# Softmax attention and a two-layer MLP: the key layout of the third batch, and every load at the second step

## The chip, the cores and the metric

The kernel runs on one core of one Trainium2 chip. The core's engines have a queue each and run side by side: TensorE (PE, matrix products, results in PSUM), VectorE (DVE), ScalarE (ACT), GpSimd (POOL) and SyncE (SP, which here only issues DMAs). The metric is the device time of one execution in microseconds (us), lower is better.

## The reference

Inputs are float32. There are 8 batches of 12 heads with 448 tokens of 64 numbers; the MLP has a width of 768 and 2048 hidden units.

```python
def _attn_ref(q, k, v):
    scale = 1.0 / np.sqrt(q.shape[-1])
    scores = scale * np.matmul(q, k.transpose(0, 1, 3, 2))
    scores = scores - np.max(scores, axis=-1, keepdims=True)
    attn = np.exp(scores)
    attn = attn / (np.sum(attn, axis=-1, keepdims=True) + 1e-09)
    return np.matmul(attn, v).astype(np.float32)

def _moe_ref(x, w_in, w_out):
    h = x @ w_in
    g = np.maximum(0.01 * h, h)
    return (g @ w_out).astype(np.float32)
# x of the MLP: the attention output of each token, its 12 heads side by side
```

## The kernel before

A unit is one batch and a pair of heads, so there are 8 x 6 = 48 units (NU), six (HP) to a batch; unit u belongs to batch u // 6. For a unit the kernel does the following.

- **Load.** POOL's DMA queue brings q, k and v of two units at a time (L157, `load_soft`) and turns them to bf16 on the way.
- **Cast.** POOL copies them into the layouts that PE needs (`cast`): q and k into one of three buffers `qkb` (L184, or L186 to L188 for the new form of k), v into `v_old` (L190) or `v_sb` (L193 to L195). `v_old` is not a buffer of its own: it lies in `x_mix`.
- **Turn.** q and k are transposed into one of four buffers `qkT`: by PE up to unit 14 (L289, copied out of PSUM by DVE at L293), by a DMA transpose from SP's queue from unit 15 (NPE) on (L271, `dma_transposes`).
- **Scores.** PE multiplies keys with queries (L309 old form, L312 new form) into one of three PSUM buffers ("slots", two heads wide), ACT takes the exponential (L321, L324, L326) into `e`.
- **Rows.** PE multiplies the exponentials with v, which has a column of ones for the sum (`pairs`, L352, old form; `weighted`, L333 and L340, new form); DVE takes the reciprocal and multiplies (L875, L876) and gives x.
- **x is turned** into `xT`, mostly by a DMA transpose from SP's queue (L267).

There are two forms of a unit. In the **old form** (units below HY, here 2 x HP = 12) the 448 keys lie in four chunks of 112, and each chunk is done for both heads: eight score products, four exponentials of 896 columns, 32 products for the rows. In the **new form** the keys lie in three chunks of 128 for both heads, and a rest of 64 keys of each head, which shares one product with the other head's: seven score products, three exponentials of 896 columns and one of 448, 28 products for the rows. The new form needs two loads for k and two for v, and three copies for each cast of k and v.

The tokens go through the MLP in seven ranges (`cuts`: 0, 640, 1152, 1664, 2176, 2688, 3072, 3584). The head (L419) and the neck (L715) do the first layer of range 0; `second(0)` does its second layer (L674, L609); `hidden(i)` (L537) and `second(i)` (L609) do the later ranges. These later products are done with fewer multiplications, from sums and differences of blocks, which DVE makes: `mix_x_part` (L484) writes `x_mix` from `xT` for the next range, in two parts, and the steps L614, L617 keep and join the partial outputs. Outputs are stored from SP's queue (L397).

Attention units are interleaved into the MLP's product stream by a planner, `place`, at the time of building: it holds a model of when slots come free and puts at each step, into PE's fixed order, a **burst** (three chunks' scores and exponentials), a **tail** (the rest chunk), or the rows of a unit. In the old form a burst is the next three chunks in a row, so four bursts are three units; in the new form it is one unit's three chunks, and the tail follows. `plan` says how many bursts each range's second layer takes (6 in `second(0)`), `goals` gives two to the neck. All queues keep the order in which the builder issues, so an instruction that waits holds up what stands behind it on its engine: POOL's casts behind its loads, SP's x turns behind its qkT turns and stores.

Within `second` and `hidden`, `advance` (called at every second or fourth step) casts the next unit and issues the next load, at every second call or, in range 0, at each; `turn_next` issues the next qkT turn. In the neck `feed` does so.

Of the kernel before, what the change touches and what calls it, by code (L numbers as in the profile page):

```python
# [16 lines left out]
def kernel(  # L17
# [9 lines left out]
    nc = tc.nc  # L27

    B, H, S, D = q.shape
    DM, DF = moe_w_in.shape  # L30
    P = 128
    HP = H // 2
    SC = 112
    NSC = S // SC
# [3 lines left out]
    NU = B * HP  # L38
# [40 lines left out]

    NV = 4  # L80
    KC = S // P
    HY = 2 * HP
    v_all = v_pool.tile([P, NV, 2 * KC + 2, D + 1], BF16, name="v")
    v_sb = [v_all[:, i] for i in range(NV)]

# [9 lines left out]
    NQ = 4  # L95
    qkT_all = qk_pool.tile([P, NQ, 2, NSC, P], BF16, name="qkT")
    qkT = [qkT_all[:, i] for i in range(NQ)]
    NB = 3
    qkb_all = cast_pool.tile([P, NB, 2, NSC, 2, D], BF16, name="qkb")
    qkb = [qkb_all[:, i] for i in range(NB)]  # L100
# [16 lines left out]
    h = h_pool.tile([P, MD, (KEEP + 1) * P], BF16, name="h")  # L117
# [15 lines left out]
    for t in (w_in_mix, w_mix):  # L133
        t = t.rearrange("p x k n -> p (x k n)")
# [42 lines left out]
    def cast(u, parts=(0, 1, 2), by=nc.gpsimd.tensor_copy):  # L177
        if u >= NU:
            return
        for x in parts:  # L180
            f = raw[u].pop(x)
            t = qkb[u % NB]
            if x < 2 and (x == 0 or u < HY):
                by(t[:SC, x].rearrange("p so h d -> p h so d"), f)  # L184
            elif x == 1:
                by(t[:, 1, :KC].rearrange("p so h d -> p h so d"), f[:, :, :KC])  # L186
                by(t[:D, 1, KC, 0], f[:D, 0, KC])
                by(t[D:, 1, KC, 1], f[:D, 1, KC])  # L188
            elif u < HY:
                by(v_old[:, u % NV, :, :, :D], f)  # L190
            else:
                t = v_sb[u % NV]
                by(t[:, :2 * KC, :D].rearrange("p (h so) d -> p h so d", h=2), f[:, :, :KC])  # L193
                by(t[:D, 2 * KC, :D], f[:D, 0, KC])
                by(t[D:, 2 * KC + 1, :D], f[:D, 1, KC])  # L195
# [68 lines left out]
    NPE = HP + 9  # L264

    def turn(dst, src):
        nc.sync.dma_start_transpose(out=dst.rearrange("p (c s) -> p c s", s=SC), in_=src)  # L267

    def dma_transposes(u):
        if NPE <= u < NU:  # L270
            nc.sync.dma_start_transpose(  # L271
                out=qkT[u % NQ].rearrange("p i c s -> p (i c) s"),
                in_=qkb[u % NB].rearrange("p i so h d -> p (i so h d)"),
            )
# [5 lines left out]
    def transposes(u, bank=None):  # L280
        if u >= min(NPE, NU):
            return
        n = SC if u < HY else P
        t, flat = qkb[u % NB], qkT[u % NQ].rearrange("p i c s -> p (i c s)")[:, :2 * NSC * n]
        for parts in ((1,), (0,)) if u == 0 else ((0, 1),):
            tr = turn_tile(bank)[:, :2 * NSC * n].rearrange("p (i s) -> p i s", i=2)
            for i in parts:
                for so in range(NSC):
                    nc.tensor.transpose(tr[:, i, ts(so, n)], t[:n, i, so].rearrange("p h d -> p (h d)"), ident[:n, :n])  # L289
            if u == 0 and parts == (0,):  # L290
                stay_warm(5)
            at = slice(parts[0], parts[-1] + 1)
            (nc.scalar.copy if u == 0 and parts == (1,) else nc.vector.tensor_copy)(  # L293
                flat.rearrange("p (i s) -> p i s", i=2)[:, at], tr[:, at]
            )
        if HY - NB <= u < HY:
            nc.vector.memset(qkb[u % NB][:, 1, KC], 0.0)

    sc_t = {}

# [524 lines left out]
    chunk = NSC * HP + 3  # L825
    nxt = HY
    owed_t = []
    rows_done = HP
    to = {"pe": HP + 2, "turn": NPE, "q": HP + 4, "cast": HP + 4, "v": HP + 4, "load": [HP + 8] * 3}
    tick = 0  # L830

    def advance(i):
        nonlocal tick
        tick += 1
        u = to["cast"]
        if u < min(NU, to["turn"] + 2, to["load"][0], to["load"][1]):
            cast(u, (0, 1))
            to["cast"] += 1
        u = to["v"]
        if u < min(NU, rows_done + NV, to["load"][2]):  # L840
            cast(u, (2,))
            to["v"] += 1
        if tick % 2 == 0 or i == 0:
            x = min(range(3), key=lambda x: to["load"][x])
            u = to["load"][x]
            if u < NU and u - 3 < (to["cast"], to["cast"], to["v"])[x]:
                load_soft(u, 2, (x,))
                to["load"][x] += 2

    def turn_next(i):  # L850

        u, full = to["turn"], nxt - len(owed_t)
        left = need[min(i + 2, NR)] - rows_done
        calm = left < 1 or left > 1 and full - rows_done < 2
        if (calm or u <= nxt + 1) and u < min(NU, full + NQ, to["cast"]):
            dma_transposes(u)
            to["turn"] += 1

# [105 lines left out]
            dma_transposes(u + 2 + r)  # L964
            to["turn"] = max(to["turn"], u + 3 + r)

    plan = [6, 6, 6, 6, 6, 4, 0]
    model = {"now": 0.0, "act": 0.0, "free": {}, "ready": {}}

    def place(i, want, soon=0, full=True, calm=True, first=False, lazy=0, keen=NU, cap=NU):  # L970

        free, ready = model["free"], model["ready"]
        done, state = 0, 0
        while True:
            settle_x(model["now"])
            now = model["now"]
            old = chunk < NSC * HY
            last, full_to = ((chunk + 2) // NSC, chunk // NSC) if old else (nxt, nxt - len(owed_t))
            whole = rows_done < full_to
            at = [free.get(id(x), 0.0) for x in slots]  # L980
            u = to["pe"]
            if full and max(want, soon) > done and u <= min(last, NPE - 1) and state == 0:
                transposes(u)
                to["pe"] += 1
                state = 1
                model["now"] += 0.45
                continue
            if want > done and state < 2 and last < NU and not owed_t and turned(last) and rows_done > last - NE and len(slots) == 3 and all(
                x <= now + 0.05 + 0.2 * j for j, x in enumerate(at)
            ):  # L990
                state = 2
                order = list(slots)
                g = chunk // 3 if old else 4 + nxt
                burst(lazy)
                if first:
                    feed(g)
                done += 1
                for x, t in enumerate(order):
                    model["act"] = max(model["act"], now + 0.45 + 0.2 * x) + 0.8
                    free[id(t)] = model["act"] + (0.3, 0.15 + 0.5 * (lazy > 1), 0.15 + 0.5 * lazy)[x]  # L1000
                    if old and (3 * g + x) % NSC == KC:
                        ready[(3 * g + x) // NSC] = model["act"] + 0.1
                model["now"] = now + 0.78
                continue
            u = to["pe"]
            if first and full and state == 0 and u < min(NPE - 1, to["cast"] - 1) and u - NQ < full_to and model["act"] <= now + 0.6:
                transposes(u)
                to["pe"] += 1
                state = 1
                model["now"] += 0.45  # L1010
                continue
            u = rows_done
            if calm and whole and not (lazy and late) and at[0] <= now + 0.05 and ready.get(u, 0) <= now + 0.05 and (
                u <= ((chunk + 5) // NSC if old else nxt + 1) - NE or u < keen
            ) and u < cap:
                t = slots[0]
                rows()
                if first:
                    pay()
                model["now"] = now + (1.08 if u < HY else 1.04)  # L1020
                free[id(t)] = model["now"] + 1.25
                continue
            if owed_t and not late and at[0] <= now + 0.05:
                t, u = slots[0], owed_t[0]
                tail(lazy)
                model["act"] = max(model["act"], now + 0.45) + 0.43
                free[id(t)] = model["act"] + 0.15 + 0.5 * (lazy > 1)
                ready[u] = model["act"] + 0.1
                model["now"] = now + 0.19
                continue  # L1030
            return done

    def second(i):
# [4 lines left out]
        for c in range(len(spots(i)[1])):  # L1038
            whole = c < plain(i)
            for x, _ in enumerate((plain_pair if whole else block_pair)(i, c)):  # L1040
                fine = 1 if whole else 2
                if x % (2 * fine) == 0:
                    advance(i)
                if c or x:
                    model["now"] += 0.65 / fine
                left -= place(i, left, calm=whole or x not in ((1, 2, 3) if i == 5 else (1, 2)), keen=need[min(i + 2, NR)], cap=NU if all(summed) else need[i + 2])
# [44 lines left out]
        pass  # L1091
    for i in range(1, NR):
        for step, _ in enumerate(hidden(i)):
            advance(i)
            if owed_t and step == 0:
                tail()
            if step % 4 == 2 and rows_done < nxt:
                rows()
            turn_next(i)
        model.update(now=0.0, act=2.3, free={id(x): 0.9 if cuts[i + 1] - cuts[i] == 4 * P and i + 1 < NR else 1.2 for x in slots}, ready={})  # L1100
        second(i)
# [30 lines left out]
```

## Time and profile before

| What | us |
|---|---|
| Median of three runs | 388.58 |
| Lowest and highest of them | 385.97, 389.38 |
| The profiled execution, its own time | 386.52 |
| Its span in the trace | 384.70 |
| PE busy in the span | 373.3 (97%) |
| ACT, DVE, POOL busy | 253.1, 230.8, 189.8 |
| PE in 0 to 61, idle | 4.1 of 61.0 |
| PE in 61 to 108.28 (end of the head, the neck, `second(0)`), idle | 3.4 of 47.3 |
| PE in 344.60 to 384.70, idle | 3.4 of 40.1 |

PE busy counts matrix products, whose ends are modelled from a pipeline; a row of products one behind the other counts as busy without a gap. PE's granted clock was 1.00 in each of these stretches.

### The profile page before, as it was taken

Reading aid. Unit: us, or ns where it says so; the run is one execution under the profiler, and the core shown is the slowest. Engines: PE = TensorE matmul, PEld = TensorE weight load, DVE = VectorE, ACT = ScalarE, POOL = GpSimd, SP = SyncE. Lnnn points to the kernel's source line nnn. Section 1 sums busy time; section 2 is a strip of 40 time slices with the busy share of each in tenths; the row PEclk is TensorE's granted clock in tenths of the full one; section 3 lists DMA queues with packets and bytes.
Section 4 is the critical chain, followed back from the end, with each engine's and each line's share of the span. In section 5 each row is a group of like instructions: output and inputs, shape, how many; then the busy total and the mean of one; then the engine's idle time right before and its main releaser. Section 6 shows DMA issues by size and latency. Waiting matters only on the chain.

```text
span 384.7 us, 9849 instructions
## 1 busy us (share of the span) xinstructions
PE 373.3 (97%) x3910; PEld 261.8 (68%) x3910; DVE 230.8 (60%) x491; ACT 253.1 (66%) x391; POOL 189.8 (49%) x403
## 2 busy tenths in 40 slices
PE   7999999989989999999999999999999999999996
PEld 3665557755578665786568875678756896668854
DVE  5663948453675836668467574565745665474854
ACT  6988875666638787378783787827878378608700
POOL 8996952898779629481285903848036100000000
PEclk9999999999999999999999999999999999999999
DMA  9999999889989929992699913999239700331022
GB/s 162 197 200 203 178 203 167 99 114 184 183 116 179 140 55 152 224 133 38 78 174 209 140 19 76 165 213 142 26 69 182 164 14 2 76 97 43 2 77 86
DMA packets 100349, 47.92 MB, mean 125 GB/s; under 512 B 65872, under 2 KB 96976, under 8 KB 100304
## 3 DMA queue, kind: packets, MB, share of 16 engines
q0 software_dynamic: 40864, 22.47, 48.0%
q1 hardware_dynamic: 59376, 24.81, 33.4%
q8 instruction: 30, 0.49, 0.5%
q14 instruction: 15, 0.12, 0.1%
q10 hardware_dynamic: 64, 0.02, 0.0%
HBM read 45.61 MB, written 11.01 MB: 147 GB/s over the span
## 4 chain that ended last, share of the span: by engine, by line
PE 72%; DMA 15%; POOL 9%; issue 2%; DVE 1%; ACT 0%; POOLq 0%; DVEq 0%
PE g L609 28%; PE g L537 14%; PE sc L537 14%; PE sc L312 6%; PE sc L340 6%; DMA w_out_sb<-in_moe_w_out_dram 4%; DMA w_in_sb<-in_moe_w_in_dram 3%; DMA xT<-x 3%; DMA w_mix<-in_v_dram 2%; POOL qkb L184 2%; PE sc L333 2%; DMA w_in_mix<-in_v_dram 2%; DMA fk<-in_k_dram 1%; POOL fv L157 1%; POOL qkb L186 1%
## 5 line engine op out<-in xcount | busy, mean ns | idle before, releaser
L321 ACT ACTIVATE e<-sc 128x896 bf16<-128x896 f32 (+1 forms) x144 | 123.7, 932 | 35.1 <-PE sc L312 29.7
L609 PEld LDWEIGHTS <-h 128*128 128x128 bf16 x632 | 59.2, 98 | 46.8 <-issue 11.7
L609 PE MATMUL g<-w_out_sb,h 128*128 128x384 bf16 x416 | 78.8, 326 | 0.4 <-DVE o L614 0.4
L184 POOL COPY qkb<-fq 112x512 bf16<-112x512 bf16 x36 | 24.0, 667 | 84.4 <-DMA qkT<-qkb 72.6
L526 ACT ACTIVATE h<-c 128x512 bf16<-128x512 f32 (+1 forms) x72 | 43.6, 613 | 25.0 <-DVE c L552 15.7
L537 PEld LDWEIGHTS <-w_in_sb 128*128 128x128 bf16 x576 | 54.3, 98 | 5.9
L537 PEld LDWEIGHTS <-w_in_mix 128*128 128x128 bf16 x432 | 41.2, 98 | 4.1
L875 DVE RECIPROCAL rec<-sc 112x8 f32<-112x8 f32 x42 | 8.7, 207 | 55.4 <-PE sc L340 41.4
L312 PE MATMUL sc<-qkT 64*128 64x448 bf16 (+1 forms) x252 | 39.3, 352 | 1.5 <-DMA qkT<-qkb 1.5
L609 PE MATMUL g<-w_mix,h 128*128 128x384 bf16 (+1 forms) x208 | 39.1, 323 | 1.4 <-DVE o L617 1.4
L340 PE MATMUL sc<-v,e 128*128 128x65 bf16 x864 | 40.0, 193 | 0.0
L340 PEld LDWEIGHTS <-e 128*128 128x128 bf16 x864 | 37.4, 98 | 2.1 <-issue 0.5
L614 DVE COPY o<-g 128x384 f32<-128x384 f32 x49 | 27.1, 553 | 11.2 <-PE g L609 10.8
L333 PE MATMUL sc<-v,e 128*128 128x130 bf16 x144 | 31.7, 220 | 0.2 <-POOL v L195 0.2
L617 DVE TENSOR_TENSOR o<-o,g 128x384 f32<-128x384 f32 x39 | 21.6, 554 | 14.9 <-PE g L609 14.1
L876 DVE TENSOR_TENSOR x<-sc,rec 112x512 bf16<-112x512 f32 x42 | 29.0, 692 | 1.7 <-DVE rec L875 0.3
L549 ACT COPY c<-g 128x512 f32<-128x512 f32 (+1 forms) x12 | 6.8, 570 | 34.6 <-PE g L537 34.6
L537 PE MATMUL sc<-xT,w_in_sb 128*128 128x256 bf16 (+1 forms) x216 | 28.5, 268 | 0.0
L537 PE MATMUL g<-xT,w_in_sb 128*128 128x256 bf16 (+1 forms) x216 | 28.5, 268 | 0.0
L157 POOL DMA_DIRECT2D fv<-in_v_dram x36 | 22.2, 624 | 9.2 <-POOL v L195 3.3
L193 POOL COPY v<-fv 128x384 bf16<-128x384 bf16 x36 | 18.6, 518 | 12.2 <-issue 8.3
L312 PEld LDWEIGHTS <-qkT 64*128 64x128 bf16 (+1 forms) x252 | 11.3, 94 | 16.9 <-issue 10.1
(129 smaller groups left out, 669.1 us busy)
## 6 DMA issues: line engine op xcount, KB each, us to landing
fq<-in_q_dram POOLq DMA_DIRECT2D x18, 224.0 KB, 5.7
w_in_sb<-in_moe_w_in_dram POOLq DMA_DIRECT2D x4, 768.0 KB, 11.3
w_out_sb<-in_moe_w_out_dram POOLq DMA_DIRECT2D x4, 768.0 KB, 15.4
out_dram<-o SPq DMA_DIRECT2D x7, 336.0 KB, 3.9
fk<-in_k_dram POOLq DMA_DIRECT2D x18, 128.0 KB, 5.1
fv<-in_v_dram POOLq DMA_DIRECT2D x18, 128.0 KB, 4.7
out_dram<-o SPq DMA_DIRECT2D x8, 288.0 KB, 3.3
fk<-in_k_dram POOLq DMA_DIRECT2D x18, 96.0 KB, 5.0
```

The lines of the kernel that those rows point to most:

```text
L157: nc.gpsimd.dma_start(out=t[p, :n, :, :so].rearrange("p u h so d -> p (u h) (so d)"), in_=(q, k, v)[x][b, hs, keys].rearrange("h (p so) d ...
L184: by(t[:SC, x].rearrange("p so h d -> p h so d"), f)
L312: nc.tensor.matmul(ps[:, j, :S].rearrange("p (so s) -> p so s", so=NSC), t[p, 1, c], t[p, 0, :, :SC], start=True, stop=True,)
L321: nc.scalar.activation(e[:, :, c, :], ps[:n, :, :S], AX.Exp, scale=scale)
L333: nc.tensor.matmul(ps, e[:, EM + qc * SC:EM + qc * SC + P], vt[:, 2 * KC:].rearrange("p j d -> p (j d)"), start=True, stop=False, skip_gro ...
L340: nc.tensor.matmul(ps[:, j * (D + 1):(j + 1) * (D + 1)], e[:, at:at + P], vt[:, j * KC + c], start=False, stop=(c == KC - 1), skip_group_c ...
L526: nc.scalar.activation(hs[:, m:m + 2, cols], x.rearrange("p (m t) -> p m t", m=2), AX.Prelu, alpha=0.01)
L537: nc.tensor.matmul(ps[:, j * nh:(j + 1) * nh], w[:, kk, ts(j, P)], x[:, kk], start=(first and j == 0 and kk == 0), stop=(kk == KH - 1), sk ...
L609: nc.tensor.matmul(ps[:, cols], x[:, m], w[:, m], start=(first and m == 0), stop=(m == MH - 1), skip_group_check=True,)
L614: by(o[:, at], ps[:, :NW])
L617: nc.vector.tensor_add(o[:, at], o[:, at], ps[:, :NW])
L876: nc.vector.tensor_mul(x, ps[:, :, :, :D], rec.to_broadcast([SC, 2, 2 * NP, D]))
```

## The change

HY becomes 3 x HP = 18: the six units 12 to 17, the third batch, are taken in the old form. With it:

- their q and k are turned with 112 partitions: on PE for 12 to 14, and by a DMA transpose of 112 partitions and eight blocks for 15 to 17;
- the zeroing of the rest chunk in the three `qkb` buffers, ahead of the first units in the new form, moves from DVE (behind PE's transposes of units 9 to 11) to POOL (into the casts of k of units 18 to 20);
- `turn_next` counts chunks instead of units as long as bursts are in the old form;
- `second(0)` takes eight bursts instead of six: six bursts are left of units 13 to 17 when the neck is done, and then units 18 and 19 follow, as they did before;
- loads are issued at every second call of `advance` in range 0 too.

```diff
--- before.py
+++ after.py
@@ -79,7 +79,7 @@
 
     NV = 4
     KC = S // P
-    HY = 2 * HP
+    HY = 3 * HP
     v_all = v_pool.tile([P, NV, 2 * KC + 2, D + 1], BF16, name="v")
     v_sb = [v_all[:, i] for i in range(NV)]
 
@@ -183,6 +183,8 @@
             if x < 2 and (x == 0 or u < HY):
                 by(t[:SC, x].rearrange("p so h d -> p h so d"), f)
             elif x == 1:
+                if u < HY + NB:
+                    nc.gpsimd.memset(t[:, 1, KC], 0.0)
                 by(t[:, 1, :KC].rearrange("p so h d -> p h so d"), f[:, :, :KC])
                 by(t[:D, 1, KC, 0], f[:D, 0, KC])
                 by(t[D:, 1, KC, 1], f[:D, 1, KC])
@@ -267,7 +269,12 @@
         nc.sync.dma_start_transpose(out=dst.rearrange("p (c s) -> p c s", s=SC), in_=src)
 
     def dma_transposes(u):
-        if NPE <= u < NU:
+        if NPE <= u < HY:
+            turn(
+                qkT[u % NQ].rearrange("p i c s -> p (i c s)")[:, :2 * S],
+                qkb[u % NB][:SC].rearrange("p i so h d -> p (i so h d)"),
+            )
+        elif NPE <= u < NU:
             nc.sync.dma_start_transpose(
                 out=qkT[u % NQ].rearrange("p i c s -> p (i c) s"),
                 in_=qkb[u % NB].rearrange("p i so h d -> p (i so h d)"),
@@ -293,8 +300,6 @@
             (nc.scalar.copy if u == 0 and parts == (1,) else nc.vector.tensor_copy)(
                 flat.rearrange("p (i s) -> p i s", i=2)[:, at], tr[:, at]
             )
-        if HY - NB <= u < HY:
-            nc.vector.memset(qkb[u % NB][:, 1, KC], 0.0)
 
     sc_t = {}
 
@@ -829,7 +834,7 @@
     to = {"pe": HP + 2, "turn": NPE, "q": HP + 4, "cast": HP + 4, "v": HP + 4, "load": [HP + 8] * 3}
     tick = 0
 
-    def advance(i):
+    def advance():
         nonlocal tick
         tick += 1
         u = to["cast"]
@@ -840,7 +845,7 @@
         if u < min(NU, rows_done + NV, to["load"][2]):
             cast(u, (2,))
             to["v"] += 1
-        if tick % 2 == 0 or i == 0:
+        if tick % 2 == 0:
             x = min(range(3), key=lambda x: to["load"][x])
             u = to["load"][x]
             if u < NU and u - 3 < (to["cast"], to["cast"], to["v"])[x]:
@@ -849,10 +854,11 @@
 
     def turn_next(i):
 
-        u, full = to["turn"], nxt - len(owed_t)
+        u, old = to["turn"], chunk < NSC * HY
+        full, last = (chunk // NSC, (chunk + 2) // NSC) if old else (nxt - len(owed_t), nxt)
         left = need[min(i + 2, NR)] - rows_done
         calm = left < 1 or left > 1 and full - rows_done < 2
-        if (calm or u <= nxt + 1) and u < min(NU, full + NQ, to["cast"]):
+        if (calm or u <= last + 1) and u < min(NU, full + NQ, to["cast"]):
             dma_transposes(u)
             to["turn"] += 1
 
@@ -964,7 +970,7 @@
             dma_transposes(u + 2 + r)
             to["turn"] = max(to["turn"], u + 3 + r)
 
-    plan = [6, 6, 6, 6, 6, 4, 0]
+    plan = [8, 6, 6, 6, 6, 4, 0]
     model = {"now": 0.0, "act": 0.0, "free": {}, "ready": {}}
 
     def place(i, want, soon=0, full=True, calm=True, first=False, lazy=0, keen=NU, cap=NU):
@@ -990,7 +996,7 @@
             ):
                 state = 2
                 order = list(slots)
-                g = chunk // 3 if old else 4 + nxt
+                g = chunk // 3
                 burst(lazy)
                 if first:
                     feed(g)
@@ -1040,7 +1046,7 @@
             for x, _ in enumerate((plain_pair if whole else block_pair)(i, c)):
                 fine = 1 if whole else 2
                 if x % (2 * fine) == 0:
-                    advance(i)
+                    advance()
                 if c or x:
                     model["now"] += 0.65 / fine
                 left -= place(i, left, calm=whole or x not in ((1, 2, 3) if i == 5 else (1, 2)), keen=need[min(i + 2, NR)], cap=NU if all(summed) else need[i + 2])
@@ -1091,7 +1097,7 @@
         pass
     for i in range(1, NR):
         for step, _ in enumerate(hidden(i)):
-            advance(i)
+            advance()
             if owed_t and step == 0:
                 tail()
             if step % 4 == 2 and rows_done < nxt:
```

## The prediction

> **What bounds the kernel now.** I read the busy time by stage first, cut where the matrix products change (head to 61, neck and first range to 108.28, range 1, ranges 2 to 5, last range). PE is nearly always at work:
>
> ```profile
> core 0: us, PE busy (x) PEld busy (x) DVE busy (x) ACT busy (x) POOL busy (x), PEclk, DMA share, GB/s
> 0.00:61.00 61.00, 56.92 (x729) 34.25 (x730) 35.89 (x94) 49.55 (x68) 47.40 (x82) 1.00 1.25 192
> 61.00:108.28 47.28, 43.84 (x461) 28.93 (x459) 27.94 (x60) 28.19 (x42) 35.80 (x71) 1.00 1.02 144
> 108.28:157.48 49.20, 48.76 (x493) 34.89 (x492) 30.57 (x60) 33.78 (x52) 33.24 (x76) 1.00 1.00 133
> 157.48:344.60 187.12, 187.12 (x1949) 136.06 (x1947) 113.82 (x236) 125.86 (x201) 73.42 (x174) 1.00 0.72 109
> ```
>
> From 157.48 to 344.60 PE has no idle time at all. PE's order in the built changed kernel is the same as before up to 53 us (two transposes there become 112 wide) and again from 108.28 on. So what the change can win lies in the second window, where PE is idle for 47.28 - 43.84 = 3.44 us. The waits of that window, from 61 to 110, name them (total, times, longest):
>
> ```profile
> DVE x_mix L484 <- DMA xT<-x: 1.9, 1, 1.9
> ...
> PE sc L312 <- DMA qkT<-qkb: 1.5, 2, 1.2
> ...
> PE g L609 <- DVE o L617: 1.4, 1, 1.4
> ...
> PE sc L333 <- POOL v L195: 0.2, 1, 0.2
> PE sc L289 <- ACT e L321: 0.2, 1, 0.2
> ```
>
> 1.5 + 1.4 + 0.2 + 0.2 = 3.3: nearly all of it. The 1.5 us are the scores of units 16 (1.25, at 86.80) and 17 (0.26, at 91.71), whose transposed q and k landed late. The timeline of POOL shows why: in the chain of waits POOL follows POOL without a break from 65.39 to 88.9.
>
> ```profile
> 65.39 0.73 POOL L184 COPY qkb<-fq 112x512 bf16<-112x512 bf16 x1 [10.57 <-PE g L715]
> ...
> 79.87 1.33 POOL L184 COPY qkb<-fq 112x512 bf16<-112x512 bf16 x1
> ...
> 82.01 0.27 POOL L188 COPY qkb<-fk 64x64 bf16<-64x64 bf16 x1
> ...
> 84.67 1.46 POOL L188 COPY qkb<-fk 64x64 bf16<-64x64 bf16 x1
> ```
>
> The casts of unit 16 end at 82.28, its DMA transpose is issued at 82.30 and scores start at 86.80; unit 17's casts end at 86.13 and its scores start at 91.71. The 1.44 us of L609 are DVE's: it waits 1.89 us for a transposed x (unit 16's, issued at 100.09, behind an output store on SP), and the join that PE needs is queued behind.
>
> **PE work.** Scores: a full group of three chunks takes 0.67 us (chain rows, six matmuls), a rest 0.18 (83.91 to 84.09). Old form: four chunks 4/3 x 0.67 = 0.89; new form 0.67 + 0.18 = 0.85. Weighted sums: 32 matmuls from 52.12 to 53.15, 1.03 us; 28 from 95.94 to 96.91, 0.97. So +0.04 and +0.06 for each of six units: +0.6 us, on the path. PE transposes of 112 and 128 both take 0.49 (45.78 to 46.27, 60.48 to 60.97): 0.
>
> **ACT.** 4 x 0.966 against 3 x 0.920 + 0.556: +0.55 a unit, +3.3 us. In 64.30 to 108.28 ACT is busy 27.42 of 43.98 us, so 16.6 us of idle time hide it; without that cover it would cost all 3.3. The order now holds ten groups and two rests there instead of eight and eight.
>
> **POOL.** A unit's casts: q and k in two copies of 0.667 and v in one of 0.618, 1.95 us, against 0.667 + (0.549 + 0.288 + 0.314) + (0.518 + 0.239 + 0.273) = 2.85. Loads of a pair: three issues of about 0.71 (2.15) against 0.717 + 4 x 0.627 = 3.22. Six units and three pairs: 5.4 + 3.2 = 8.6 us less. Three memsets come in from DVE, where they took 0.11; no POOL memset of that size is in the view, so 0.1 to 0.7 each (the smallest by DVE's, the largest by a copy four times as wide), taken as 0.3. They stand ahead of the k casts of units 18 to 20, when POOL is ahead; so 0.
>
> Now the chain from 65.39, which starts when q of unit 14 lands behind the w_out loads (the same bytes, so the same time): casts of 14 and 15 2.67, v 0.62, loads of 16/17 2.15, two v 1.24, loads of 18/19 3.22 (new form), casts of 16 1.33, v 0.62, casts of 17 1.33, and about 1 us of gaps: 14.2. Unit 16 is ready at 77.6 (was 82.28), unit 17 at 79.6 (was 86.13).
>
> At 84.67 L188 took 1.46 us (median 0.233) beside two two-input DVE operations (L440, 85.02 to 86.04), and L187 1.44 at 90.59 beside the next two. If that hits unit 17's casts once more, it is ready at 80.8; the margin below bears it.
>
> **When PE needs it.** I lay the new PE order from 64.3 with the rows' rates (0.0835 a neck matmul, 0.163 a 384-wide one): groups at 64.3, 68.0, 73.8, 76.5, 81.8, 84.5, 88.8, 93.4, 96.0, 100.2. Unit 16's first chunk is second in the sixth group (84.7), unit 17's third in the seventh (89.2). With a landing of 4.5 (the six x turns of 66 to 100 had 4.1 to 6.2, a qkT turn of this stage a median of 5.4) they land at 82 and 84. So 1.5 us go. The margins are 2.6 and 5 us.
>
> SP's queue: x of units 13 and 14 now stands behind the turns of 16 and 17, and x of 16 and 17 stands behind the turn of 20, which waits for the seventh group. Weighted sums of 16 come at 92, its x is turned at 93.4 and lands by 98.5 to 99.6; DVE reaches the mixing at about 100. So the 1.44 us of L609 go too. The 0.2 of v and most of the 0.2 of the slot go by the shorter POOL chain. Kept: 0.4 us for new small waits of this order (bound 0 to 1). The loads that came every step and now come every second step move to range 1, where POOL waits long for qkT turns (5.85 us at 144.07): 0.
>
> **Sum.** -(3.4 - 0.4) + 0.6 = -2.4 us. The profiled execution took 386.52 (span 384.70 and 1.82 around it), so 384.1. The median shown is 388.58, 2.06 more, and the runs go from 385.97 to 389.38. If that surplus lies outside this window, the changed median is 386.2; if it is more of the same waits, 384.1. I take the middle, 385.0 (-0.9%).
>
> **Rivals.** (1) The idle time only moves. v of the old form lies in x_mix, which the mixing for range 1 overwrites, and unit 17's weighted sums now come 5.3 us before range 1 (before: 97.10 to 108.28, 11.2). From their end to the first product with the mixed second part is 5.3 + 1.0 + 4 x 0.66 = 8.9 us. My chain is 1.2 (DVE) + 5 (turn) + 1 (three mixing steps) = 7.2. For: before, the last mixing step ended at 109.8, 12.7 us after those sums. Against: there, two stores and another turn were ahead on SP. If it stays at 12.7 minus the last step's 0.3, PE stalls 3.5 and all is given back: 387.6 against the profiled base of 386.5; with the surplus of the median up to 389.7. Chance 0.18.
>
> The mixing steps L484 took 0.248 to 0.485 us over all their shapes, so rows show them held up by 0.2 at most. The Trainium skill, page "SBUF — State Buffer", section "Who interferes with whom", says that a DVE instruction with two SBUF inputs and a GpSimd instruction that reads SBUF shut each other out for a whole instruction. The POOL copies above agree (1.2 us lost each time). By that rule each of the three steps could wait for a POOL cast of 0.667, the chain would be 9.2 instead of 7.2, PE would stall 0.3, and my sum would be -2.1; it is a part of why this rival keeps 0.18.
>
> (2) Slower: the turn of 112 partitions by 8 blocks. No row has it. x turns are 112 by 4 and land in 4.7, qkT turns 128 by 8 in 5.4, so I took that range; the worst landing of an x turn in the view of xT is 10.9. Above 7.1 us unit 16 is late. At 10.9 each, one behind the other, unit 17 would land at 77.6 + 21.8 = 99.4 instead of 89.2: PE stalls 10.2, 394.3. It decides for "slower by 1%" from about 10 us. Against: x turns with 112 partitions are not slow, and 896 rows of 256 bytes are moved instead of 1024. With other waits of the same place (ACT with three score buffers), chance 0.17.
>
> (3) The change does not what it says: the order does show six units in four chunks and the single loads, so 0.03 for no effect of any sort.
>
> **How the numbers follow.** My case has 0.62; its times are 384.1 to 386.2, with up to 1.6 less if the kept waits and the PE terms are smaller, 382.5. About 1% is what a measurement of this kernel can tell: below 384.7 is faster, above 392.5 slower. I give 0.42 of the 0.62 to faster, because the surplus of the median is most likely in the POOL-paced stage, and 0.20 to same; rival 1 is same (0.18), rival 2 slower (0.17), the rest is split. Range 382.5 to 389.7, my case and rival 1 (0.80).
>
> **What would show it.** Right: from 61 to the end of the first range PE's idle time falls from 3.44 to under 1 us, no wait of scores for qkT and none of L609 for the join, PE busy there up 0.6, ACT up 3, POOL's casts of units 16 and 17 done by about 80, and every later stage unchanged to 0.1 us. Wrong: scores waiting for a qkT turn with landings over 7 us (rival 2), or range 1's products waiting for DVE's mixing (rival 1), or idle time in the windows that I took as unchanged.

## The result, and the profile after

The changed kernel takes 383.51 us (median of six runs, 381.98 to 386.25), the kernel before 388.35 us (median of six, 385.97 to 389.38). The ratio of the means is 0.9889 (that of the medians 0.9875) with a 95% interval of 0.9845 to 0.9933: faster by 1.1%. The ratios in this document leave out executions that are more than 1.5% longer than the fastest of the same kernel. The forecast was 385.0 with a range of 382.5 to 389.7. The profiled execution of the changed kernel took 383.68 us, its span is 381.3 us.

The busy time by stretch comes first. The cuts lie at the first scores of the neck and at the first product of range 1 (L537 before, L542 now), since these two points can be found to a hundredth in every kernel of this study. Columns as before: stretch, length, then busy time and count of PE, PEld, DVE, ACT, POOL, the granted clock, DMA. Before:

```profile
0.00:64.31 64.31, 60.23 (x760) 36.81 (x760) 39.16 (x101) 50.32 (x69) 47.40 (x82) 1.00 1.26 192
64.31:108.28 43.97, 40.53 (x428) 26.38 (x427) 24.66 (x53) 27.42 (x40) 35.80 (x71) 1.00 0.99 140
108.28:384.70 276.42, 272.55 (x2725) 198.66 (x2723) 166.97 (x339) 175.40 (x282) 106.66 (x250) 1.00 0.69 106
```

After:

```profile
0.00:65.04 65.04, 61.30 (x761) 36.98 (x762) 38.64 (x98) 50.39 (x69) 44.32 (x72) 1.00 1.25 189
65.04:105.50 40.46, 40.43 (x458) 26.39 (x458) 25.78 (x52) 29.55 (x40) 30.03 (x55) 1.00 1.07 146
105.50:381.30 275.80, 272.31 (x2725) 198.66 (x2723) 166.71 (x339) 175.04 (x282) 106.86 (x249) 1.00 0.67 107
```

The middle row is the one that the prediction was about: 43.97 us became 40.46, and PE's idle time in it 43.97 - 40.53 = 3.44 became 40.46 - 40.43 = 0.03. POOL does 5.8 us less there, ACT 2.1 us more. The first row is 0.73 longer and the last 0.62 shorter; both come up below.

PE's waits over the whole span after (in total, times, longest). All of them lie before 61 us (the wait for qkT among them is for a turn by PE, which DVE copies out); behind 61 us no wait for qkT and none for a join is left.

```profile
PE g L234 <- DVE gate L229: 1.2, 1, 1.2
PE sc L314 <- ACT e L326: 0.6, 3, 0.2
PE g L296 <- ACT qkb L257: 0.5, 1, 0.5
PE sc L314 <- DVE qkT L300: 0.5, 1, 0.5
PE sc L357 <- ACT c L329: 0.4, 1, 0.4
PE g L389 <- DVE x L370: 0.3, 1, 0.3
PE sc L314 <- ACT h L701: 0.2, 1, 0.2
```

POOL's timeline shows why (start, length, operation, how often; in brackets the idle time ahead of it and what ended it):

```profile
66.52 0.61 POOL L184 COPY qkb<-fq 112x512 bf16<-112x512 bf16 x1 [15.62 <-DMA fq<-in_q_dram]
...
72.47 0.70 POOL L157 DMA_DIRECT2D fv<-in_v_dram  x1
...
77.37 0.67 POOL L184 COPY qkb<-fq 112x512 bf16<-112x512 bf16 x1
77.92 0.66 POOL L184 COPY qkb<-fk 112x512 bf16<-112x512 bf16 x1
...
79.52 0.61 POOL L184 COPY qkb<-fq 112x512 bf16<-112x512 bf16 x1
80.08 0.61 POOL L184 COPY qkb<-fk 112x512 bf16<-112x512 bf16 x1
80.64 0.61 POOL L184 COPY qkb<-fq 112x512 bf16<-112x512 bf16 x1
81.19 0.20 POOL L187 MEMSET qkb<- 128x128 bf16 x1
```

The chain starts 1.1 us later than before (66.52 against 65.39) and is nevertheless through with unit 16 at 78.6 (before: 82.28) and with unit 17 at 80.7 (86.13): each k and v of units 14 to 17 is one copy, and each load of units 16 and 17 one issue. In the summary of the chain that ended last POOL and PE have changed places; before it was `PE 72%; DMA 15%; POOL 9%`, and after:

```profile
PE 83%; DMA 12%; POOL 3%; issue 1%; ACT 0%; DVE 0%; POOLq 0%; DVEq 0%
```

### The profile page after: what moved, and what is told of

It reads as the page before. It is cut to its first block, busy times and chain, and to the rows that moved or that the text cites. A ratio compares the mean times of both kernels' runs of the same rounds, so it can differ in the third digit from the quotient of the medians.

```text
span 381.3 us, 9889 instructions
## 1 busy us (share of the span) xinstructions
PE 374.0 (98%) x3940; PEld 262.0 (69%) x3940; DVE 231.1 (61%) x488; ACT 255.0 (67%) x391; POOL 181.2 (48%) x376
## 4 chain that ended last, share of the span: by engine, by line
PE 83%; DMA 12%; POOL 3%; issue 1%; ACT 0%; DVE 0%; POOLq 0%; DVEq 0%
PE g L614 32%; PE g L542 14%; PE sc L542 14%; PE sc L317 7%; PE sc L345 6%; DMA w_out_sb<-in_moe_w_out_dram 5%; PE g L679 3%; DMA o<-in_k_dram 3%; DMA w_mix<-in_v_dram 2%; PE g L720 2%; DMA w_in_mix<-in_v_dram 2%; PE sc L357 2%; PE sc L338 2%; PE sc L314 1%; POOL w_in_mix L157 1%
## 5 line engine op out<-in xcount | busy, mean ns | idle before, releaser
L614 PEld LDWEIGHTS <-h 128*128 128x128 bf16 x632 | 59.3, 98 | 44.6 <-issue 9.2
L614 PE MATMUL g<-w_out_sb,h 128*128 128x384 bf16 x416 | 78.7, 326 | 0.0
L542 PEld LDWEIGHTS <-w_in_sb 128*128 128x128 bf16 x576 | 54.3, 98 | 5.9
L542 PEld LDWEIGHTS <-w_in_mix 128*128 128x128 bf16 x432 | 41.2, 98 | 4.1
L614 PE MATMUL g<-w_mix,h 128*128 128x384 bf16 (+1 forms) x208 | 39.0, 323 | 0.0
L345 PE MATMUL sc<-v,e 128*128 128x65 bf16 x720 | 33.3, 193 | 0.0
L317 PE MATMUL sc<-qkT 64*128 64x448 bf16 (+1 forms) x210 | 32.8, 352 | 0.0
L345 PEld LDWEIGHTS <-e 128*128 128x128 bf16 x720 | 31.2, 98 | 1.4
L542 PE MATMUL sc<-xT,w_in_sb 128*128 128x256 bf16 (+1 forms) x216 | 28.5, 268 | 0.0
L542 PE MATMUL g<-xT,w_in_sb 128*128 128x256 bf16 (+1 forms) x216 | 28.5, 268 | 0.0
L338 PE MATMUL sc<-v,e 128*128 128x130 bf16 x120 | 26.5, 221 | 0.0
L157 POOL DMA_DIRECT2D fv<-in_v_dram x33 | 20.6, 630 | 3.4 <-POOL v L197 2.1
L188 POOL COPY qkb<-fk 128x384 bf16<-128x384 bf16 x30 | 16.4, 547 | 10.9 <-DMA fk<-in_k_dram 10.9
L314 PE MATMUL sc<-qkT 64*128 64x448 bf16 x144 | 20.2, 362 | 1.3 <-ACT e L326 0.6
```

The costliest lines, as they stand in the source:

```text
L157: nc.gpsimd.dma_start(out=t[p, :n, :, :so].rearrange("p u h so d -> p (u h) (so d)"), in_=(q, k, v)[x][b, hs, keys].rearrange("h (p so) d ...
L314: nc.tensor.matmul(ps[:, j, :S], t[p, S + c * SC:S + c * SC + P], t[p, :S], start=True, stop=True)
L317: nc.tensor.matmul(ps[:, j, :S].rearrange("p (so s) -> p so s", so=NSC), t[p, 1, c], t[p, 0, :, :SC], start=True, stop=True,)
L338: nc.tensor.matmul(ps, e[:, EM + qc * SC:EM + qc * SC + P], vt[:, 2 * KC:].rearrange("p j d -> p (j d)"), start=True, stop=False, skip_gro ...
L345: nc.tensor.matmul(ps[:, j * (D + 1):(j + 1) * (D + 1)], e[:, at:at + P], vt[:, j * KC + c], start=False, stop=(c == KC - 1), skip_group_c ...
L542: nc.tensor.matmul(ps[:, j * nh:(j + 1) * nh], w[:, kk, ts(j, P)], x[:, kk], start=(first and j == 0 and kk == 0), stop=(kk == KH - 1), sk ...
```

## The experiments

The theory: POOL's serial chain of casts and loads sets when units 16 and 17 are turned; through SP's order (the turn of unit 20 stands ahead of the turns of x of 16 and 17) it also sets when DVE can mix, and so when the joins come that PE waits for. The change wins by taking work off that chain. Rivals: the rhythm of the loads, the number of DMA issues, the changed layout by itself on PE and ACT, and chance in one profile.

**Only the rhythm of the loads, on the kernel before.**

```diff
-        if tick % 2 == 0 or i == 0:
+        if tick % 2 == 0:
```

> Kernel before with only the loads of the first range at every second step; PE's order is unchanged. Theory (the gain comes from POOL's shorter casts and loads of units 12 to 17, and from x of 16 and 17 being turned and mixed in another order): the waits of scores for qkT (1.5 us) and of PE for the join (1.4 us) stay, because the loads that move stand behind the casts of unit 17; PE idle from 61 us to the start of range 1 stays at 2.8 to 3.8 us, ratio 0.997 to 1.003. Rival (the loads at each step kept POOL busy): the idle time falls under 1.5 us and the ratio to 0.993 or less.

Measured: ratio 0.9998 (0.9956 to 1.0041). No gain. The profiled execution (394.66 us) is one of those left out, so nothing is read from its profile: whether PE's idle time stayed as expected is not shown.

**The rhythm taken back, on the changed kernel.** `advance(i)` and `tick % 2 == 0 or i == 0` again.

> Changed kernel with the loads of the first range at each step again; PE's order is unchanged. Theory (POOL's shorter casts and loads of units 12 to 17 are what frees PE; the cadence of the loads is not): PE idle from the first group of the neck to the start of range 1 stays under 0.6 us, though POOL's cast of unit 20 may move by up to 3 us. Rival (the cadence made the gain): one of the old waits comes back, idle 1.5 us or more.

Measured: 381.9 us in its one run. The window is that of the changed kernel to a hundredth, though POOL is busy there for 34.92 us, 4.9 more:

```profile
63.77:104.23 40.46, 40.43 (x457) 26.30 (x457) 25.27 (x52) 29.58 (x40) 34.92 (x58) 1.00 1.10 149
```

So the loads that are issued behind the casts of 16 and 17 cost nothing here, and the rhythm is no part of the gain.

**The casts and loads made as dear as before, in the changed kernel.** The products, exponentials and turns stay those of the changed kernel; k and v of units 12 to 17 are copied in three pieces and loaded in two.

```diff
+                if x == 1 and u >= 12:
+                    by(t[:SC, 1, :KC].rearrange("p so h d -> p h so d"), f[:, :, :KC])
+                    by(t[:SC, 1, KC, 0], f[:, 0, KC])
+                    by(t[:SC, 1, KC, 1], f[:, 1, KC])
...
+                if u >= 12:
+                    by(v_old[:, u % NV, :, :KC, :D], f[:, :, :KC])
+                    by(v_old[:, u % NV, 0, KC, :D], f[:, 0, KC])
+                    by(v_old[:, u % NV, 1, KC, :D], f[:, 1, KC])
...
+                (slice(0, D), NSC, slice(0, NSC * D)), (slice(D, SC), NSC, slice(NSC * D, S)),
+            ) if x > 0 and 12 <= u < HY else (
```

> Changed kernel with POOL's old cost put back for units 12 to 17: k and v cast in three copies each, and loaded in two issues each, the bytes and PE's order unchanged. Theory (POOL is the cause): casts of unit 16 end about 3.5 us later than in the changed kernel, at 82, its turn lands at about 87 where PE needs it at 86.1; the cast of unit 20 and with it the turn of 20 on SP, behind which x of 16 stands, are 3 to 4 us later, so the mixing and the joins wait too: PE idle in the stage 0.8 to 2.5 us, ratio 0.992 to 0.997. Rival (the order of PE's groups made the gain): idle under 0.4 us, ratio 0.986 to 0.991.

Measured: ratio 0.9962 (0.9932 to 0.9992). By these ratios about two thirds of the gain are gone, with nothing changed but POOL's work; where the last third lies is not shown. The wait that came back is the join's, not qkT's. From the list of PE's waits, and from the timeline of DVE (L501 is the mixing, L634 the join):

```profile
PE g L626 <- DVE o L634: 2.2, 1, 2.2
```

```profile
105.25 0.43 DVE L501 TENSOR_TENSOR x_mix<-xT 128x512 bf16<-128x512 bf16 x1 [3.54 <-DMA xT<-x]
105.59 0.55 DVE L634 TENSOR_TENSOR o<-o,g 128x384 f32<-128x384 f32 x1
```

DVE waits 3.54 us for the turned x, and the join stands behind. Back along the queues: that x was issued by SP at 99.01, behind the turn of unit 20 at 96.07, which waited for POOL's casts of unit 20 (95.0 to 96.1). Ahead of these casts POOL had itself waited 3.75 us for the load of that k. It had issued the load at 87.96, in the changed kernel at 86.12, and the casts start at 95.00 instead of 91.79: 1.8 us of the delay are POOL's, 1.4 the load's landing. In the changed kernel the turn of 20 is issued at 92.78, x of 16 at 95.30, and DVE finds it there at 102.02.

**Casts and loads one at a time.** The first two parts of the diff above alone (the casts), and the third alone (the loads).

> The changed kernel, but each cast of k and of v of units 12 to 17 is cut into three copies on POOL (as the new form needs them); the loads stay single. My theory (POOL's chain of casts and loads sets when units 16 and 17 are turned, and through the turn of unit 20 and the turns of x of 16 and 17 on SP also when the join of L614/L622 comes): of the 5.4 us that the casts cost more, 3.6 lie ahead of the end of unit 17's casts and all of it ahead of unit 20's; so most of what came back with casts and loads together (ratio to the kernel before 0.996) comes back here: ratio 0.991 to 0.997, PE idle in the neck and the first range 0.5 to 2.2 us, ending at DVE's join. Rival (the number of DMA issues is what counts, not POOL's copies): nothing comes back, 0.987 to 0.991, idle under 0.3.

> The changed kernel, but each load of k and of v for units 12 to 17 is issued in two pieces; the casts stay single. My theory: only the pieces of one pair of units (1.1 us of POOL's time) lie between the start of POOL's chain and the casts of units 16 and 17, and the margin there is larger: little comes back, ratio 0.987 to 0.992, PE idle in the neck and the first range under 0.5 us. Rival (the number of DMA issues is what counts): the ratio is that of casts and loads together, 0.996, with the join of DVE waited for.

Measured: casts in pieces 0.9926 (0.9886 to 0.9966); loads in pieces 0.9891 (0.9816 to 0.9966), beside 0.9889 for the change as it is. The intervals overlap, so the ratios alone do not tell the casts from the rest; the waits do. With the loads in pieces PE has no wait behind 61 us. With the casts in pieces:

```profile
PE sc L324 <- DMA qkT<-qkb: 1.3, 1, 1.3
PE g L624 <- DVE o L632: 1.2, 1, 1.2
```

That is 2.5 us of idle time, a little over the 0.5 to 2.2 expected, and the same two waits as in the first profile of the kernel before (1.5 and 1.4). The windows of neck and first range tell the parts from each other (casts in pieces, loads in pieces, both):

```profile
64.43:107.80 43.37, 40.77 (x458) 26.20 (x458) 26.32 (x52) 29.66 (x40) 32.86 (x72) 1.00 1.10 137
64.59:105.04 40.45, 40.42 (x457) 26.29 (x457) 27.72 (x52) 29.55 (x40) 30.80 (x57) 1.00 1.06 141
64.64:108.48 43.84, 41.58 (x457) 26.61 (x457) 25.96 (x52) 29.58 (x40) 34.55 (x75) 0.98 1.03 134
```

The casts alone make the window as long as it is in the kernel before (42.98 to 43.97 in its three profiles), the loads alone leave it as it is in the changed kernel (40.46); with both, 1.0 of the 43.84 us are a lower clock (last section). By chance POOL's chain starts earlier or later against PE's first scores of the neck, but that does not explain the difference: with the loads in pieces and with both it starts alike (0.75 and 0.76 us ahead), and with the casts in pieces it starts late (1.67 us behind), as in the changed kernel (1.48). So the copies are what counts, and there are 3.6 us of them ahead of unit 17 against 1.1 us of issues. What dear loads cost when the chain starts late is not shown. And the ten executions with the casts in pieces spread from 383.14 to 387.57 us, the profiled one (385.82) among the longer ones: its profile shows what can come back, not what comes back each time.

**POOL's loads put off, in the kernel before.** If POOL is late, loads of units 18 and 19 could wait until the casts of 16 and 17 are done.

```diff
-            if n and u <= ahead and u - 3 < to[y]:
+            if n and u <= ahead and u - 3 < to[y] and u < 18:
```

> Kernel before, its layout kept, with the loads of units 18 and 19 (five issues, 3.2 us of POOL) behind the casts of unit 16 instead of ahead of them. Theory: casts of unit 16 end by about 79 instead of 82.3, those of 17 by 83 to 84, and both qkT waits (1.25 and 0.26 us) go; the join's 1.4 us stays; a wait for the turns of 18 or 19, whose loads are now late, of up to 1 us may come in. PE idle in the stage 1.8 to 2.9 us instead of 3.4. Rival (the layout itself, or PE's order, removed the waits): the qkT waits stay within 0.5 us of 1.5.

Measured: 396.61 us in its one run. The qkT waits went, as expected, and the time got worse. PE's waits, and the lines of DVE behind them:

```profile
PE g L609 <- DVE o L617: 9.4, 1, 9.4
PE sc L333 <- POOL v L195: 2.2, 1, 2.2
```

```profile
113.57 0.43 DVE L484 TENSOR_TENSOR x_mix<-xT 128x512 bf16<-128x512 bf16 x1 [9.86 <-DMA xT<-x]
...
114.39 0.42 DVE L484 TENSOR_TENSOR xT<-xT 128x512 bf16<-128x512 bf16 x1
114.72 0.55 DVE L617 TENSOR_TENSOR o<-o,g 128x384 f32<-128x384 f32 x1
```

The loads put off delay the casts of 18, 19 and 20; SP's turn of 20 goes out at 105.75, x of 16 and 17 behind it at 108.17. POOL's work had been moved, not removed, and the wait moved to the end of the same path.

**The mixing placed later, alone and with the loads put off.** The planner's due time for the mixing in the first range, in the kernel before:

```diff
-                        fresh[y] = model["now"] + 7.0
+                        fresh[y] = model["now"] + (9.0 if i == 0 else 7.0)
```

> Kernel before, its layout kept, with the mixing of x for range 1 put 2 us later by the planner's clock, so that the joins stand ahead of it in DVE's queue. Theory: the wait of L609 for the join (1.44 us) goes, and so do the 0.4 us at the start of range 1 or they stay; range 1 has at most 0.5 us of new waits for the mixing; the qkT waits (1.5 us) stay. PE idle in the stage 1.7 to 2.3 us. Rival (x of unit 16 is turned too late for any order): PE waits as much at range 1 for the mixed x, 1 us or more.

> Kernel before, its layout kept, with both: loads of 18 and 19 behind the casts of 16, and the mixing later. Theory: the two gains add; PE idle from 61 us to the start of range 1 0.3 to 1.5 us, range 1 no longer than 49.1; ratio 0.990 to 0.995, near the changed kernel's 0.989. Rival (the layout is needed): idle above 2 us, ratio above 0.996.

Measured: alone 387.61 us in its one run, no change that can be told. The wait at the join is 0.6 us, but one for v of 1.8 us is there, and the waits for qkT, which I had expected to stay, are not. Together with the loads put off: ratio 1.0181 (1.0145 to 1.0217), where I had expected a gain. Again it is x of unit 16, 7.1 us late for DVE, and PE waits 6.1 us for the join. I had counted only the casts of 16 and 17 as POOL's debt; those up to unit 20 belong to it too.

**POOL relieved in the layout of the kernel before: v of units 13 to 15 cast by DVE.** This asks whether the other layout is needed at all.

```diff
-            cast(owed_v[0], (2,))
+            cast(owed_v[0], (2,), nc.vector.tensor_copy if owed_v[0] in (13, 14, 15) else nc.gpsimd.tensor_copy)
```

> Kernel before, layout and cadence kept, with only the v casts of units 13, 14 and 15 done by DVE instead of POOL (nine copies, 3.1 us of POOL; no load is deferred). Theory: unit 16 is ready by about 79 instead of 82.3 and the qkT waits go; everything behind it on POOL comes 3 us earlier, the cast of 20 too (93.9 waits for its load, so by 1 to 3), so x of 16 is turned 1 to 3 us earlier and the join's wait shrinks from 1.4 to 0 to 1; PE idle in the stage 0.5 to 1.8 us, ratio 0.991 to 0.996. Rival (only the old form of units 12 to 17, with its order, removes the waits): idle 2.5 us or more, ratio 0.998 or more.

Measured: ratio 1.0146 (1.0110 to 1.0182), slower, for a reason that I had not seen: DVE works in order too, and waited 6.80 us for the load of v, with the x (L875, L876) that PE needed behind it. From the list of PE's waits (that of L614 lies near the end of range 1), and the window of neck and first range:

```profile
PE sc L384 <- DVE x L876: 7.2, 1, 7.2
...
PE g L609 <- DVE o L614: 0.8, 1, 0.8
```

```profile
73.68:114.37 40.69, 40.23 (x428) 26.34 (x427) 22.01 (x51) 27.38 (x40) 26.68 (x54) 1.00 0.94 135
```

The stall lies ahead of the window; in it, with the layout and the order of PE those of the kernel before, there are 40.69 us (before 43.97, changed kernel 40.46). POOL's chain had begun at 63.60, 10.1 us ahead of the first scores (before: 1.1 us behind them), mostly because of the stall, besides the casts that it was spared. So the waits go in the old layout too when POOL is ahead, and the change of layout is one way to get there. But PE's stall had let DVE, SP and the loads get ahead as well; POOL alone ahead was not tried.

**Both kernels profiled again**, to see what is chance.

> The kernel before, profiled again. Open is where the 2 us lie by which its median (388.4) is above its first profiled execution (386.52). Theory: in the same place, the neck and the first range, since POOL's chain starts when a load lands and so stands earlier or later against PE by chance: an execution that is 2 us longer has 2 us more PE idle time between its first scores of the neck and the first product of range 1 (3.4 us in the first profile), and the rest of the span (384.70 less 43.97) stays within 0.7 us. Rival: the surplus lies elsewhere (the start, the end, what is outside the span); then the idle time stays near 3.4.

> The same once more: the theory has idle time of neck and first range rise and fall with the time, 1 us for 1 us; the rival has it stay near 3.4 us.

> The changed kernel, profiled again. Theory: its idle time from the first scores of the neck to the first product of range 1 stays under 0.5 us (0.03 in its first profile), whatever the start-up did, so that the stretch takes 40.4 to 41. Rival (the first profile was a lucky one): 1 to 3 us of waits for qkT or the join come back.

Measured: 387.80 and 387.44 us before, 383.46 after. The changed kernel repeats: 40.54 us in the window, 0.02 of it idle. Of the kernel before my theory fell: its longer executions have less idle time in the window, not more.

```profile
65.92:108.90 42.98, 40.49 (x427) 26.35 (x427) 25.30 (x55) 27.38 (x40) 35.71 (x69) 1.00 1.04 137
```

Here PE comes to the neck 1.6 us later and POOL's chain starts 1.5 us earlier (63.88), so the scores find qkT ready, and the idle time is mostly a join wait of 2.1 us. The extra time came in ahead of the window. From PE's waits of this run:

```profile
PE g L609 <- DVE o L617: 2.1, 1, 2.1
PE sc L309 <- DVE x L876: 1.4, 1, 1.4
...
PE g L609 <- DVE o L614: 0.9, 1, 0.9
```

x of L876 was late because two sums of DVE ahead of it took 2.94 us instead of 1.37 (first profile of before) or 1.43 (after), while POOL copied without a pause from 44.20:

```profile
43.47 2.94 DVE L454 TENSOR_TENSOR w_in_mix<-w_in_sb,w_in_mix 128x768 bf16<-128x768 bf16 x2
```

```profile
44.20 1.20 POOL L190 COPY x_mix<-o 112x512 bf16<-112x512 bf16 x2
45.31 0.63 POOL L184 COPY qkb<-fq 112x512 bf16<-112x512 bf16 x1
45.86 0.90 POOL L186 COPY qkb<-fk 128x384 bf16<-128x384 bf16 x1
```

The Trainium skill, page "SBUF — State Buffer", section "Who interferes with whom", has a DVE instruction with two SBUF inputs and a GpSimd instruction that reads SBUF hold each other up for a whole instruction, whoever comes first; the 1.5 us lost here agree with it. In the first profile of before POOL made the same copies beside these sums, and there the copies were the longer ones (the first two rows 1.62 and 0.93 us instead of 1.20 and 0.63). In the changed kernel POOL casts with two copies at that place instead of four, and the wait is in neither of its profiles. The number of copies alone is not the reason: with the casts in pieces there are four again, and the two sums took 1.46 us. Which meets which seems to be chance.

**One measure for all profiles.** How long x of unit 16 lay ready before SP issued its turn tells the profiles apart. In the five without a join wait up to the start of range 1 (the changed kernel twice, the rhythm taken back, the loads in pieces, v on DVE) it was 0.03 to 1.7 us. In the eight with one (the kernel before three times, the casts in pieces, both, the three runs with loads put off or the mixing later) it was 2.5 to 13.4 us. So the wait at the end of the path, in either layout, goes with SP's queue ahead of that x.

## Why the prediction came out right, and where it was off

The means of the three profiles before and the two after, cut at the scores behind ACT's L696 (31 to 32 us), the first scores of the neck and the first product of range 1:

| Stretch | Before | After | Difference |
|---|---|---|---|
| start, to the scores behind L696 | 31.56 | 32.42 | +0.86 |
| from there to the neck | 33.80 | 32.60 | -1.20 |
| neck and first range | 43.34 | 40.50 | -2.84 |
| range 1 to the end | 276.77 | 275.79 | -0.98 |
| span | 385.47 | 381.30 | -4.17 |

- **POOL, 8.6 us less** (5.4 of casts, 3.2 of loads): 189.8 to 181.2, as forecast. To a tenth that is chance: as means of the three profiles before and the two after it is 191.3 to 180.4. The casts of 16 and 17 were laid to end at 77.6 and 79.6 from a start at 65.39, 12.2 and 14.2 us on; from the start at 66.52 they took 12.1 and 14.2. The memsets took 0.20 each (0.3 taken).
- **The 3.44 us of idle time go, 0.4 come back**: right in its first half and by the named path; of the 0.4 only 0.03 came. The three turns of 112 by 8 landed in 2.9 to 5.5 us, median 5.2 (4.5 taken), and the margins bore it. That disposes of rival 2, the slow turn of 112 by 8.
- **x of 16 turned at 93.4 and there at 98.5 to 99.6**: it was issued at 95.30, 1.9 later, of which 0.7 is the later start of the stage, and DVE found it ready at 102.02. Rival 1 did not come: no range-1 product waited for the mixing. But its mechanism is the one that the experiments brought out. Where POOL's work came back or was put off, PE's wait for a join, behind DVE's wait for xT, cost 2.2, 6.1 and 9.4 us, and 1.2 of 2.5 us with the casts in pieces.
- **PE +0.6 us, all in this window**: PE's busy time in it fell by 0.10 in place of rising. Part of the 40.53 before was not work: with v on DVE and POOL ahead, the same products kept PE busy for 40.23. Against that the changed kernel has 0.20 more. The term was mis-sized by 0.4 to 0.7.
- **ACT +3.3 us, hidden**: +2.1, hidden. Exponentials overlap in ACT, so mean lengths overstate them: in the profile of before the 108 of 920 ns keep it busy for 91.9 us, not 99.4.
- **Range 1 and after unchanged to 0.1 us**: wrong, by 0.6 to 1.3 us in our favour. In each profile of before, PE waits 0.4 to 0.9 us for the join of L614 near the end of range 1, once more behind a mixing step that waits for xT (1.45 us in the second profile of before, 0.20 after). That wait is gone after, and it is absent too in the runs that put the cost of POOL's casts, loads or both back, so it is not that cost that makes it. That turns and stores are earlier on SP may be the reason; it was not tried. I had treated the later stages as decoupled since PE's order there is the same.
- **The 2 us by which the median lies above the first profile, "most likely in the POOL-paced stage"**: this step failed. The two further profiles, 1.28 and 0.92 us longer than the first, have 1.0 and 0.9 us less in that stage and 1.1 us more between 32 us and the neck. Part of the rest may be the clock (last section). The middle that I took, 385.0, was 1.5 too high, because the changed kernel shows no such surplus: its median lies at its profiled time.
- **The time.** The sum of -2.4 us became -3.4 in the span of the first two profiles (384.7 to 381.3). Of the 4.17 us between the means, 2.84 lie in the window that the prediction was about; 1.20 and 0.98 lie in stretches that it took as unchanged, less 0.86 of a longer start. So the mechanism is right for two thirds of the gain, and that the median came within 1.5 us of the forecast is in part luck. Two slips in the working move nothing: the view of the x turns has four, not six, and the middle of 384.1 and 386.2 is 385.15.

The longer start is most likely chance, which is not shown: both profiles of the changed kernel have it (32.44 and 32.39), and the four variants of this kernel have 31.18 to 31.83 at the same place.

## What to carry to other kernels

When engines take their work in order, an engine far from its limit (POOL, at 49%) can pace one stage, and the wait that it causes shows up on another engine several queues on: follow the queues (POOL's cast, SP's turn, SP's next turn, DVE's mixing, DVE's join) before deciding which cost to cut. Removing work from the head of such a chain paid here; putting it off, or giving it to another engine that works in order, moved the wait and made it longer. And take two or three profiles of the kernel before: one showed waits for qkT that the next two did not have.

## What the runs showed of the hardware

A wait of PE can cost more than its length. In the kernel with casts and loads in pieces PE stood idle for 2.23 us; the windows behind it show the granted clock (after POOL's column):

```profile
103.96:106.19 2.23, 0.01 (x1) 0.00 (x0) 0.94 (x3) 0.78 (x2) 1.05 (x2) 1.00 1.25 159
106.19:107.30 1.11, 1.11 (x5) 0.59 (x5) 1.08 (x3) 0.00 (x0) 0.00 (x0) 0.62 1.37 175
107.30:108.48 1.18, 1.18 (x5) 0.51 (x4) 0.44 (x2) 0.00 (x0) 0.32 (x1) 0.50 1.41 178
108.48:109.77 1.29, 1.29 (x8) 0.91 (x7) 1.00 (x3) 0.00 (x0) 0.65 (x2) 0.50 0.10 16
109.77:111.50 1.73, 1.73 (x36) 1.66 (x35) 0.88 (x3) 1.17 (x2) 1.55 (x7) 0.97 0.03 9
```

The clock falls to a half and comes back after some 3.5 us. The products from 106.19 to 109.77 took 3.58 us; the same products in the changed kernel go by in 1.95 (104.20 to 106.15). So 2.23 us of waiting cost 2.23 + 3.58 - 1.95 = 3.9. After 2.12 us of waiting (second profile of before) and 2.20 us (the wait for v in both runs with loads put off) the clock stayed at 1.00; after 6.1 and 9.4 us it was at 0.50 for another 3.0 and 4.0 us. The length of one wait does not decide it: in the run with the mixing placed later the clock stood at 0.50 from 12.1 to 15.5 us, in the start, behind four waits of 0.25 to 0.78 us. The Trainium skill, page "TensorE: Matmul & The Clock Gate", Part 1, has the clock halved after an idle window of about 3.4 us, whose phase is free, and restored after a busy one as long; the restoring agrees, and in these two places the halving came after less idle time than that.

It also bears on the spread. Of 47 executions of the kernel before, 11 had a mean clock of 0.996 or less; their median is 389.77 us, that of the others 387.44. Of the six of the changed kernel, five had 1.00 and took 381.98 to 384.59, and the one at 0.99 took 386.25. A mean of 0.996 is what one such fall amounts to, half the clock for 3.4 of 385 us. In the two profiled runs with 0.996 it lay behind the join wait in one and in the start in the other; where it lay in the unprofiled executions can't be seen.
